# Query features of three tiles made inside the spatial stage, with the weight sums written over their source, and PSUM banks and one sum of the drain taken in another order

## The chip, the cores and the metric

One core of a Trainium2 chip. The metric is the device time of one execution in microseconds (us). The engines are PE (TensorE: matmuls; its weight loads are shown as PEld), DVE (VectorE), ACT (ScalarE), POOL (GpSimd) and SP (SyncE, which here only issues DMAs). Each engine works through its instructions in a fixed order; DMA queues move data beside them.

## The reference

```python
xn = layernorm(x)                                   # 2048 x 512
# A: linear attention with hedgehog features, 32 heads of 16
q, k, v   = xn @ wqkv, by heads
phi(t)    = concat(softmax(t @ w_phi), softmax(-t @ w_phi))
kv, z     = phi(k)^T v,  sum over positions of phi(k)
A         = (phi(q) kv / (phi(q) z + 1e-6)) @ wo
# B: gated MLP over positions
z1, z2    = halves of gelu(xn @ w_in)               # 2048 x 688 each
g         = w_sp @ layernorm(z2) + b_sp             # w_sp: 2048 x 2048
B         = (z1 * g) @ w_out
out       = x + A + B
```

All in fp32. The kernel splits each factor into a high part rounded to the fast matmul type and a low part (the rest), so one product takes three matmuls: L57 (high by high), L58 and L59 (with one low part). `round_h` (L49, ACT) makes the high part and `rest_l` (L53, DVE) the low one.

## The kernel before, in words

The 2048 positions are 16 tiles of 128. The work runs in four stages, and PE goes through them without overlap:

- Projections and k, q features (to about 190 us); e, the exponentials of a query tile with their sums, goes to `e_d` in HBM.
- The second half of `x @ w_in` and its layer norm (to about 290 us).
- **The spatial stage** (about 282 to 489 us): `w_sp @ z2` by Strassen and Winograd. The output is made in 8 pairs of row tiles (`i`, 0 to 7), each from 7 products P1, P2, P6, P5, P7, P3, P4 (in this order, `FORM`). A product adds up in one PSUM bank (`g`) over four steps, quarters of the columns: `n` runs over 32 steps of 42 matmuls. There are 8 banks; a pair holds 7, so P1 of the next pair gets the eighth, its P2 the bank of the old P1, and so on.
- **The final stage** (from 489 us): for each tile `project_u` (u @ w_out into `pout`), for each pair of tiles `attend` (feature transposes, `po`, `oT`) and then `project_o` (oT @ wo, added to `pout`).

For a step, `load_a(n)` loads two blocks of 256 KB of the weights (`wf`, on SP), and `prep_a(n)` makes the four sums S1 to S4 (DVE, L632 to L636, into `S`) and the high and low parts of A11, A12, S1 to S4 and A22 (tiles `A`; ACT L49, DVE L53). Two sets of `A` tiles alternate, so those of step n wait until products of step n − 2 have used them.

At the end of a pair, `drain` empties the seven banks into the tile `c` (ACT L819 copies P1, then DVE L818 to L826), and `gate` applies the gelu to z1 (tile `z1t`, ACT L832), multiplies (L835), splits off a remainder and transposes into the z1 tile (L844, L846), from where 8 DMAs on SP write `u_d` and `ur_d`. The tiles `c` and `z1` have one buffer each. `load_z1` (POOL, L800) brings the next pair's z1 when these writes have landed. After pairs 2 and 4, `c` and `z1` also serve `turn_q`: e of query tile 0 or 1 is loaded into `c` (POOL, L922), transposed by DVE (L579) and written to `q_d`.

`q_fin` turns e of a query tile into its finished features: seven DVE instructions, L563 to L570, which need e and `zb` (the normalizer z, spread over the partitions). Tiles 0 and 1 are finished before the spatial stage, tile 2 in its last steps, and later ones by `features(s)` in the final stage.

`wo` comes in 16 DMAs of 64 KB on SP (L863) and is rounded to `woh` and `wol`.

The order of each engine's instructions is set when the program is built, by a scheduler that takes what can run first; dependences by tile and buffer set the waits. `tc.issue_after` in the code orders one instruction behind another. So code that moves also moves other instructions.

Of the kernel before, what the change touches and what calls it, by code (L numbers as in the profile page):

```python
# [10 lines left out]
F32 = mybir.dt.float32  # L11
# [7 lines left out]
P = 128  # L19
# [22 lines left out]
def mixer(ctx: ExitStack, tc: tile.TileContext, x, x_t, wv, wqkT, phi_bd, wo, w_in, wst, b_r, w_out, out):  # L42
# [557 lines left out]

    def load_a(n):
        i, q = SEQ[n]
        f = []
        for k in range(2):
            t = ws.tile([P, QC, P], F32, tag=f"f{k}", bufs=2, name="wf")
            sp.dma_start(t, wst[2 * i + k, :, q * QC:(q + 1) * QC, :])
            f.append(t.rearrange("p (k two) t -> p two k t", two=2))
        return f

    def prep_a(n, f):  # L610

        a, b = f
        pl = hl[n % 2]
        ops = {}

        tiles = {}
        for names, more in ((("S3", "S4"), 0), (("A22",), 0), (("A11", "A12"), QP), (("S1", "S2"), 0)):
# [11 lines left out]
        sums = (sm[0].tile([P, 4, 2, P], F32, name="S") if sm else  # L629
                zw.tile([P, 4, FC], F32, tag=("T", "z2")[n], bufs=n + 1, name="S").rearrange("p a b -> p (a b)")[:, :8 * P].rearrange("p (a k b) -> p a k b", a=4, k=2))  # L630
        parts(("A11", "A12"), a)
        dve.tensor_tensor(sums[:, 0], b[:, 0], b[:, 1], op=ALU.add)  # L632
        dve.tensor_tensor(sums[:, 1], sums[:, 0], a[:, 0], op=ALU.subtract)  # L633
        parts(("S1", "S2"), sums[:, 0:2])
        dve.tensor_tensor(sums[:, 2], a[:, 0], b[:, 0], op=ALU.subtract)
        dve.tensor_tensor(sums[:, 3], a[:, 1], sums[:, 1], op=ALU.subtract)  # L636
        parts(("S3", "S4"), sums[:, 2:4])
        parts(("A22",), b[:, 1:2])
        return ops

    hl, raw, A, sm = [ws, None], {}, {}, []
    NE = 2
    with ExitStack() as p1:
        tmp1 = p1.enter_context(left("tmp1", 1))
        kvT = tmp1.tile([P, D], F32, name="kvT")
        zb = tmp1.tile([P, NF], F32, name="zb")
        zhl = tmp1.tile([P, 4, D], F32R, tag="zhl", name="zhl")
        psk = p1.enter_context(psum("psk", 2))

        def make_zb():  # L650

            ones_r = tmp1.tile([P, P], F32R, name="ones_r")
            round_h(act, ones_r, ones)
            for k in range(2):
                pz = psk.tile([P, D], F32, tag="kvt", name="pz")
                cs = slice(k * D, (k + 1) * D)
                h, l = (zhl[:, 2 * k + n] for n in range(2))
                round_h(act, h, zacc[:, cs])
                rest_l(l, zacc[:, cs], h)
                pe.matmul(pz, ones_r, h, start=True, stop=False)  # L660
                pe.matmul(pz, ones_r, l, start=False, stop=True)
                dve.tensor_copy(zb[:, cs], pz)

        def make_kvT():
            kvm = zw.tile([P, 4, FC], F32, tag="T", name="kvm").rearrange("p a b -> p (a b)")[:, :D]
# [18 lines left out]
        A[0] = prep_a(0, raw.pop(0))  # L684
        sp.dma_start(kvT_d, kvT)
# [94 lines left out]
    raw[2] = load_a(2)  # L780
    normed(*late.pop(), ins)
    ctx_zw.__exit__(None, None, None)
    ctx_zc.__exit__(None, None, None)
# [9 lines left out]
    sm.append(mid.enter_context(right("S", 1)))  # L793
    ctx_psg = psum("psg", 8)
    psg = ctx_psg.__enter__()

# [17 lines left out]
    def drain(i, g, cb):  # L814
        g = {k: t[:, :FC] for k, t in g.items()}
        b1, b2 = (bias[:, 2 * i + k:2 * i + k + 1] for k in range(2))
        c11, c12, c21, c22 = (cb[:, k, j] for k in range(2) for j in range(2))
        add = lambda o, p, b, q: dve.scalar_tensor_tensor(o, p, b, q, op0=ALU.add, op1=ALU.add)  # L818
        first = act.activation(c12, g["P1"], AF.Copy)  # L819
# [3 lines left out]
        dve.tensor_tensor(c21, g["P7"], c21, op=ALU.add)  # L823
# [76 lines left out]
    for n in range(NC):  # L900
# [4 lines left out]
        if n % NQ == NQ - 1 and i < NP - 1:  # L905
# [1 line left out]
            cq = c[:, :, :FH].rearrange("p k (j f) -> p k j f", j=2)  # L907
            cb = drain(i, g, cq)
            g = {}
        if n + 3 < NC:  # L910
            raw[n + 3] = load_a(n + 3)
        if n + 2 < NC:
            A[n + 2] = prep_a(n + 2, raw.pop(n + 2))
        if n % NQ == NQ - 1 and i < NP - 1:
# [3 lines left out]
            if i in (2, 4):  # L918
# [2 lines left out]
                        for tag, name in (("c", "c"), ("z1", "z1t")))  # L921
                pool.dma_start(e, e_d[s, :, :NF])  # L922
                turn_q(s, t, e, pool)
        if n == NC - 4:
            stage_w()
        if n == NC - 3:
# [30 lines left out]
    def er_pair(name):  # L957
        return cw.tile([P, 2, NF], F32R, tag="er", bufs=3, name=name)

    def features(s):  # L960
# [4 lines left out]
        if s == 3:  # L965
            return
# [6 lines left out]
        e = es[s]  # L973
        if s % 2 == 0:
            ep[s] = er_pair("er")
        es[s] = ep[s - s % 2][:, s % 2]
        lasts[6] = pool.dma_start(es[s].bitcast(F32), e).ins
# [14 lines left out]
    fin.append(last)  # L992
# [43 lines left out]

    def project_u(i, u):
        uh, ul, rt = u
        p = pso.tile([P, D], F32, tag="out", bufs=2, name="pout")
        for c in range(KF):  # L1040
            mm3(p, (uh[:, c], ul[:, c]), wu[c], c == 0, False)
        for k, w in enumerate(wu[KF]):
# [35 lines left out]
            rows = [(m * QP, (m + 1) * QP) for m in range(c // 2 * 8 + c % 2, (c // 2 + 1) * 8, 2)]  # L1078
            load_w(wo, rows, wo_h[:, c], wo_l[:, c], cw.tile([P, D], F32, tag="wof", bufs=4, name="wof"))
    with tc.issue_after(load_w.last):  # L1080
        ets[3] = load_q(3, slot("et"))
        for s in (2, 3):
            us[s] = fetch_u(s)
        ets[4] = load_q(4, slot("et"))

    def ahead(i):

        if i + 5 < NT:
            ets[i + 5] = load_q(i + 5, slot("et"))
        if i + 4 < NT:  # L1090
            with tc.issue_after(brought[i + 2]) if i + 6 >= NT else ExitStack():
                us[i + 4] = fetch_u(i + 4)
        if 3 < i + 3 < NT:
            features(i + 3)

    p, nxt = {}, dict(enumerate(uT))
    for i in range(0, NT, 2):
# [6 lines left out]
            p[i + 1] = project_u(i + 1, nxt.pop(i + 1))  # L1104
        if not i:
            fin.append(lasts[7])
            features(3)
# [51 lines left out]
```

## Time and profile before

| | |
|---|---|
| median of 3 runs | 623.57 us (622.28 to 623.81) |
| profiled execution | 623.54 us, of which the span of the profile is 621.8 us |
| PE busy | 607.6 us (98%) |
| DVE busy | 520.4 us (84%) |
| ACT, POOL busy | 261.3 us (42%), 135.5 us (22%) |
| spatial stage | first product at about 282 us, last one ends at 489.0 us |
| mean clock of PE | 0.991 of full speed |

The profile is of one execution. Rows of the timeline show a start in us from the span's start, a duration, the engine, the line of the kernel, what is written and read, and in brackets the idle time before and what ended it. The lists of waits show how long an engine stood in all, how often and the longest time. Buffer names are those of the program: `g` a product's bank, `c` the drained tile, `A` prepared weights, `wf` raw weights.

### The profile page before, as it was taken

To read this page: it belongs to the slowest core of one execution; us is meant where nothing else is said; L and a number is where in the kernel's file an instruction comes from. 1 tells how busy PE (TensorE), PEld (TensorE's weight loads), DVE (VectorE), ACT (ScalarE), POOL (GpSimd) and SP (SyncE) were. 2 spreads that over 40 slices of the span, in tenths; PEclk is the share of its full clock that TensorE was granted. 3 is DMA by queue.
4 is the path that set the end of the run, shared out by engine and by line. 5 is a ranking of instruction groups with operands and counts; after the bars stand their busy time and mean duration, and the time that the engine had idled before them with its cause. 6 is when DMAs were issued, how large, how long until landed. Compare 5 with 4: busy or idle time off the path is not lost.

```text
span 621.8 us, 11389 instructions
## 1 busy us (share of the span) xinstructions
PE 607.6 (98%) x4286; PEld 551.0 (89%) x4286; DVE 520.4 (84%) x929; ACT 261.3 (42%) x416; POOL 135.5 (22%) x236
## 2 busy tenths in 40 slices
PE   8999999999999999999999999999999799999996
PEld 6888888888889999999999999999999677777775
DVE  5999999999977688888899887697878889999921
ACT  5653334323523657876444442343344333332221
POOL 4122333232110025551000002001000032243420
PEclk9999999999999999999899999999999899999999
DMA  8556875665457847001463755536465799898882
GB/s 310 195 138 164 221 188 160 163 164 155 124 164 209 291 151 253 1 1 37 145 153 114 198 133 177 129 120 184 125 194 158 232 324 324 280 261 250 215 208 58
DMA packets 58414, 109.95 MB, mean 177 GB/s; under 512 B 12456, under 2 KB 24616, under 8 KB 58120
## 3 DMA queue, kind: packets, MB, share of 16 engines
q1 hardware_dynamic: 43400, 64.96, 34.4%
q0 software_dynamic: 12656, 38.64, 24.5%
q10 hardware_dynamic: 2304, 5.64, 2.4%
q8 instruction: 33, 0.54, 0.4%
q14 instruction: 21, 0.17, 0.1%
HBM read 66.85 MB, written 35.80 MB: 165 GB/s over the span
## 4 chain that ended last, share of the span: by engine, by line
PE 77%; DVE 8%; POOL 4%; ACT 4%; issue 3%; DMA 3%; SPq 0%; ACTq 0%; POOLq 0%; DVEq 0%
PE g L57 8%; PE g L58 8%; PE g L59 8%; PE proj L58 7%; PE proj L57 7%; PE proj L59 7%; PE pout L57 6%; PE pout L59 5%; PE pout L58 5%; PE zps L59 3%; PE zps L58 3%; PE zps L57 3%; DVE A L53 1%; POOL rstd L98 1%; PE po L1029 1%
## 5 line engine op out<-in xcount | busy, mean ns | idle before, releaser
L57 PE MATMUL g<-B,A 128*128 128x344 f32 x448 | 142.6, 319 | 2.0 <-ACT A L49 1.1
L58 PE MATMUL g<-B,A 128*128 128x344 f32 x448 | 142.3, 319 | 0.5 <-DVE B L53 0.5
L59 PE MATMUL g<-B,A 128*128 128x344 f32 x448 | 138.5, 318 | 0.2 <-DVE A L53 0.2
L57 PEld LDWEIGHTS g<-B,A 128*128 128x128 f32 x448 | 84.7, 189 | 3.5 <-ACT A L49 1.5
L58 PEld LDWEIGHTS g<-B,A 128*128 128x128 f32 x448 | 84.6, 189 | 0.7 <-DVE B L53 0.7
L59 PEld LDWEIGHTS g<-B,A 128*128 128x128 f32 x448 | 83.7, 189 | 0.5 <-DVE A L53 0.5
L49 ACT ACTIVATE A<-S 128x512 fp32r<-128x512 f32 x64 | 39.4, 629 | 71.0 <-DVE S L633 55.9
L57 PE MATMUL proj<-wqk_h,xT 128*128 128x512 f32 x128 | 50.1, 391 | 0.0
L59 PE MATMUL proj<-wqk_h,xT 128*128 128x512 f32 x128 | 49.8, 389 | 0.0
L58 PE MATMUL proj<-wqk_l,xT 128*128 128x512 f32 x128 | 49.8, 389 | 0.0
L124 ACT ACTIVATE e<-e,r_x 128x1024 f32<-128x1024 f32 x26 | 29.8, 1148 | 42.3 <-DVE e L123 41.2
L53 DVE TENSOR_TENSOR A<-S,A 128x512 fp32r<-128x512 f32 x64 | 42.9, 685 | 3.0 <-ACT A L49 3.0
L49 ACT ACTIVATE A<-wf 128x512 fp32r<-128x512 f32 (+1 forms) x64 | 33.0, 516 | 27.7 <-DMA wf<-in_wst 16.4
L57 PE MATMUL zps<-w1h,xT 128*128 128x344 f32 (+2 forms) x128 | 40.7, 320 | 0.0
L59 PE MATMUL zps<-w1h,xT 128*128 128x344 f32 (+2 forms) x128 | 40.7, 318 | 0.0
L58 PE MATMUL zps<-w1l,xT 128*128 128x344 f32 (+2 forms) x128 | 40.7, 318 | 0.0
L57 PE MATMUL zps<-w2h,xT 128*128 128x344 f32 (+2 forms) x128 | 40.7, 318 | 0.0
L58 PE MATMUL zps<-w2l,xT 128*128 128x344 f32 (+2 forms) x128 | 40.6, 317 | 0.0
L59 PE MATMUL zps<-w2h,xT 128*128 128x344 f32 (+2 forms) x128 | 40.3, 317 | 0.0
L53 DVE TENSOR_TENSOR A<-wf,A 128x512 fp32r<-128x512 f32 (+1 forms) x64 | 35.1, 551 | 4.3 <-ACT A L49 4.3
L127 DVE TENSOR_REDUCE sm<-e 128x64 f32<-128x1024 f32 x26 | 31.1, 1199 | 2.5 <-ACT e L124 2.5
L800 POOL DMA_DIRECT2D z1t<-z_d x16 | 8.7, 552 | 110.0 <-DMA wf<-in_wst 59.3
(222 smaller groups left out, 1441.0 us busy)
## 6 DMA issues: line engine op xcount, KB each, us to landing
wf<-in_wst SPq DMA_DIRECT2D x64, 256.0 KB, 3.5
e_d<-e POOLq DMA_DIRECT2D x16, 544.0 KB, 4.8
et<-e_d SPq DMA_DIRECT2D x16, 544.0 KB, 7.5
z_d<-z1f ACTq DMA_DIRECT2D x16, 344.0 KB, 3.2
z1t<-z_d POOLq DMA_DIRECT2D x16, 344.0 KB, 4.8
zacc<-e POOLq DMA_DIRECT2D x10, 512.0 KB, 4.9
u<-u_d SPq DMA_DIRECT2D x15, 320.0 KB, 5.5
xt<-in_x SPq DMA_DIRECT2D x16, 256.0 KB, 3.8
```

Source lines behind the costliest of these rows:

```text
L49: return act.activation(h, src, AF.Copy).ins
L53: return (eng or dve).tensor_tensor(l, src, h.bitcast(F32), op=ALU.subtract).ins
L57: pe.matmul(dst, ah, bh, start=start, stop=False)
L58: pe.matmul(dst, ah, bl, start=False, stop=False)
L59: return pe.matmul(dst, al, bh, start=False, stop=stop).ins
L98: pool.tensor_tensor(r, mv[:, 1:2], mhalf, op=ALU.pow)
L124: softmax_pair.last = less, act.activation(e, e, AF.Exp, scale=scale).ins
L127: dve.tensor_reduce(sm, heads(e), axis=AX.X, op=ALU.add)
L800: pool.dma_start(t[:, k, :FH], z1_d[2 * i + k])
L1029: lasts[3] = pe.matmul(po[r][c * QP:(c + 1) * QP, k], kvT[rows, m // 2, cols], fs[m // 4][rows, m // 2 % 2], start=True, stop=True).ins
```

## The change

1. After the gate of pairs 1, 3 and 5, the features of query tiles 2, 3 and 4 are made in the tiles `c` and `z1`: POOL loads e into `c` and zb into `z1`, DVE runs `q_fin`, and POOL writes the features back to `e_d`. Tiles 2 and 3 are loaded from there near the end of the spatial stage, tile 4 after it; `q_fin` of tile 2 leaves the last steps, `features(3)` the final stage, and later tiles are finished one tile sooner.
2. The two blocks of raw weights are one tile in three buffers (one in a new pool `fy`, for the former pool `S`), loaded four steps ahead instead of three.
3. The weight sums are written over the raw weights. The order of a step's preparation is now A22, A11 and A12, the sums, S2 and S1, S4 and S3.
4. c22 is made from P7 before c21 is finished, instead of from P5 after.
5. The pool of `pout` is opened ahead of that of the transposes, and the first `pout` is taken at once.

```diff
     def load_a(n):
         i, q = SEQ[n]
-        f = []
+        tag = "fx"[n] if n < 2 else "fyx"[(n - 2) % 3]
+        t = (fy[0] if tag == "y" else ws).tile([P, 2, QC, P], F32, tag="wf" + tag, name="wf")
         for k in range(2):
-            t = ws.tile([P, QC, P], F32, tag=f"f{k}", bufs=2, name="wf")
-            sp.dma_start(t, wst[2 * i + k, :, q * QC:(q + 1) * QC, :])
+            sp.dma_start(t[:, k], wst[2 * i + k, :, q * QC:(q + 1) * QC, :])
...
+        parts(("A22",), b[:, 1:2])
         parts(("A11", "A12"), a)
-        dve.tensor_tensor(sums[:, 0], b[:, 0], b[:, 1], op=ALU.add)
-        dve.tensor_tensor(sums[:, 1], sums[:, 0], a[:, 0], op=ALU.subtract)
-        parts(("S1", "S2"), sums[:, 0:2])
-        dve.tensor_tensor(sums[:, 2], a[:, 0], b[:, 0], op=ALU.subtract)
-        dve.tensor_tensor(sums[:, 3], a[:, 1], sums[:, 1], op=ALU.subtract)
-        parts(("S3", "S4"), sums[:, 2:4])
-        parts(("A22",), b[:, 1:2])
+        a11, a12, a21, a22 = a[:, 0], a[:, 1], b[:, 0], b[:, 1]
+        dve.tensor_tensor(a22, a21, a22, op=ALU.add)
+        dve.tensor_tensor(a21, a11, a21, op=ALU.subtract)
+        dve.tensor_tensor(a11, a22, a11, op=ALU.subtract)
+        dve.tensor_tensor(a12, a12, a11, op=ALU.subtract)
+        parts(("S2", "S1"), pair(a11, a22))
+        parts(("S4", "S3"), pair(a12, a21))
...
         dve.tensor_tensor(c12, g["P5"], c21, op=ALU.add)
+        add(c22, g["P7"], b2, c12)
         dve.tensor_tensor(c21, g["P7"], c21, op=ALU.add)
-        add(c22, g["P5"], b2, c21)
...
-        if n + 3 < NC:
-            raw[n + 3] = load_a(n + 3)
+        if n + 4 < NC:
+            raw[n + 4] = load_a(n + 4)
...
+            elif i % 2 and i < NP - 2:
+                s = NE + i // 2
+                et, t = (gt.tile([P, 2, FU], F32, tag=tag, name=name).rearrange("p k f -> p (k f)")
+                         for tag, name in (("c", "c"), ("z1", "z1t")))
+                pool.dma_start(et[:, :NF + 2 * H], e_d[s])
+                pool.dma_start(t[:, :NF], zb_d)
+                e, _ = q_fin(et[:, :QW], t[:, :NF], t[:, :NF])
+                pool.dma_start(e_d[s, :, :NF], e)
...
-            ets[2] = load_q(2, slot("et"))
-            es[2], last = q_fin(ets.pop(2), slot("qtmp")[:, :NF], zb)
+            for s in (2, 3):
+                es[s] = slot("er", F32R)[:, :NF]
+                sp.dma_start(es[s].bitcast(F32), e_d[s, :, :NF])
...
+    pso = ctx.enter_context(psum("pso", 1))
+    pout = [pso.tile([P, D], F32, tag="out", bufs=2, name="pout")]
     pst = ctx.enter_context(psum("pst", 4))
-    pso = ctx.enter_context(psum("pso", 1))
...
-        if 3 < i + 3 < NT:
-            features(i + 3)
+        if 4 < i + 4 < NT:
+            features(i + 4)
```

What this does to the order. On POOL, in the first pairs of the spatial stage, before (z1t is the tile `z1`; L800 loads z1, L922 and L581 are the turn of query tile 0; the x counts instructions that follow each other):

```order
L770 TENSOR_SCALAR nb<-mv,rstd 128x1
L800 DMA z1t<-z_d 128x688 x6
L922 DMA c<-e_d 128x1024
L581 DMA q_d<-z1t 32x4x256 x4
L800 DMA z1t<-z_d 128x688 x4
```

and now, where L931 and L932 load e and zb, and L934 writes the features back:

```order
L803 DMA z1t<-z_d 128x688 x4
L931 DMA c<-e_d 128x1088
L932 DMA z1t<-zb_d 128x1024
L803 DMA z1t<-z_d 128x688 x2
L934 DMA e_d<-c 128x1024
L925 DMA c<-e_d 128x1024
```

Three transfers through `c` and `z1` now stand between pair 1 and pair 2, with pair 2's load of z1 among them.

On DVE at the end of an even pair, before (L818, L821, L822 and L823 are the drain, L636 and L53 the preparation of the next weights; DMAHW stands for a transfer issued by SP, DMASW for one by POOL):

```order
L818 SCALAR_TENSOR_TENSOR c<-g,bias,c 128x344 [waits PE_49,Activation_49]
L636 TENSOR_TENSOR S<-wf,S 128x256 [waits DVE_49]
L53 TENSOR_TENSOR A<-wf,A 128x2x256 [waits Activation_49]
L821 TENSOR_TENSOR c<-g,c 128x344 [waits PE_49]
L822 TENSOR_TENSOR c<-g,c 128x344 [waits DVE_49,PE_49]
L53 TENSOR_TENSOR A<-S,A 128x2x256 [waits Activation_49]
L823 TENSOR_TENSOR c<-g,c 128x344 [waits DVE_49,PE_49]
```

and now, from the last of the seven instructions of `q_fin` on:

```order
L570 TENSOR_TENSOR c<-c 128x1024 [waits DVE_49]
L53 TENSOR_TENSOR A<-wf,A 128x256 [waits DMAHW6_49,Activation_49]
L635 TENSOR_TENSOR wf<-wf 128x2x128 [waits DVE_49]
L636 TENSOR_TENSOR wf<-wf 128x2x128 [waits DVE_49]
L637 TENSOR_TENSOR wf<-wf 128x2x128 [waits DVE_49]
L638 TENSOR_TENSOR wf<-wf 128x2x128 [waits DVE_49]
L53 TENSOR_TENSOR A<-wf,A 128x2x256 [waits Activation_49] x2
L821 SCALAR_TENSOR_TENSOR c<-g,bias,c 128x344 [waits DMASW2_49,Activation_49]
L824 TENSOR_TENSOR c<-g,c 128x344
```

The drain of pairs 2, 4 and 6 has moved behind the whole preparation of the second step after it, and its first instruction waits for a transfer of POOL, the write of L934; the copy of P1 on ACT waits for it too. Between L563 and L570 stand one sum and three rests of weights.

On PE at the end of the spatial stage, before:

```order
L57 MATMUL g<-B,A 128x344
L58 MATMUL g<-B,A 128x344
L59 MATMUL g<-B,A 128x344
L57 MATMUL pout<-wu,u_uh 128x512 [waits DVE_49,Activation_49]
L58 MATMUL pout<-wu,u_uh 128x512
L59 MATMUL pout<-wu,ul_rt 128x512
```

and now:

```order
L58 MATMUL g<-B,A 128x344
L59 MATMUL g<-B,A 128x344
L57 MATMUL pout<-wu,u_uh 128x512
L58 MATMUL pout<-wu,u_uh 128x512
L59 MATMUL pout<-wu,ul_rt 128x512
```

The first `pout` no longer waits for the drain.

More of the change, by code (lines that the diff above doesn't have):

```diff
@@ L602, in load_a @@
         i, q = SEQ[n]
-        f = []
+        tag = "fx"[n] if n < 2 else "fyx"[(n - 2) % 3]
+        t = (fy[0] if tag == "y" else ws).tile([P, 2, QC, P], F32, tag="wf" + tag, name="wf")
         for k in range(2):
-            t = ws.tile([P, QC, P], F32, tag=f"f{k}", bufs=2, name="wf")
-            sp.dma_start(t, wst[2 * i + k, :, q * QC:(q + 1) * QC, :])
-            f.append(t.rearrange("p (k two) t -> p two k t", two=2))
-        return f
+            sp.dma_start(t[:, k], wst[2 * i + k, :, q * QC:(q + 1) * QC, :])
+        return [t[:, k].rearrange("p (k two) t -> p two k t", two=2) for k in range(2)]
     def prep_a(n, f):
@@ L616, in prep_a @@
         tiles = {}
-        for names, more in ((("S3", "S4"), 0), (("A22",), 0), (("A11", "A12"), QP), (("S1", "S2"), 0)):
+        for names, more in ((("S4", "S3"), 0), (("A22",), 0), (("A11", "A12"), QP), (("S2", "S1"), 0)):
             tiles[names] = pl.tile([P, D * len(names) + more], F32R, tag="".join(names), name="A")
@@ L627, in parts, with pair @@
                 ops[m] = h[:, k], l[:, k]
-        sums = (sm[0].tile([P, 4, 2, P], F32, name="S") if sm else
-                zw.tile([P, 4, FC], F32, tag=("T", "z2")[n], bufs=n + 1, name="S").rearrange("p a b -> p (a b)")[:, :8 * P].rearrange("p (a k b) -> p a k b", a=4, k=2))
+        def pair(x, y):
+            (first, kd, td), more = x.ap, y.offset - x.offset
+            return bass.AP(x.tensor, x.offset, [first, [more, 2], kd, td])
+        parts(("A22",), b[:, 1:2])
         parts(("A11", "A12"), a)
-        dve.tensor_tensor(sums[:, 0], b[:, 0], b[:, 1], op=ALU.add)
-        dve.tensor_tensor(sums[:, 1], sums[:, 0], a[:, 0], op=ALU.subtract)
-        parts(("S1", "S2"), sums[:, 0:2])
-        dve.tensor_tensor(sums[:, 2], a[:, 0], b[:, 0], op=ALU.subtract)
-        dve.tensor_tensor(sums[:, 3], a[:, 1], sums[:, 1], op=ALU.subtract)
-        parts(("S3", "S4"), sums[:, 2:4])
-        parts(("A22",), b[:, 1:2])
+        a11, a12, a21, a22 = a[:, 0], a[:, 1], b[:, 0], b[:, 1]
[5 more added lines that the diff above has]
+        parts(("S4", "S3"), pair(a12, a21))
         return ops
-    hl, raw, A, sm = [ws, None], {}, {}, []
+    hl, raw, A, fy = [ws, None], {}, {}, []
     NE = 2
@@ L684, in mixer @@
         A[0] = prep_a(0, raw.pop(0))
+        raw[2] = load_a(2)
         sp.dma_start(kvT_d, kvT)
@@ L792, in mixer @@
     gt = mid.enter_context(right("gt", 1))
-    sm.append(mid.enter_context(right("S", 1)))
+    fy.append(mid.enter_context(right("fy", 1)))
+    raw[3] = load_a(3)
     ctx_psg = psum("psg", 8)
@@ L958, in er_pair, with into_pair @@
         return cw.tile([P, 2, NF], F32R, tag="er", bufs=3, name=name)
+    def into_pair(s, eng, e):
+        if s % 2 == 0:
+            ep[s] = er_pair("er")
+        es[s] = ep[s - s % 2][:, s % 2]
+        return eng.dma_start(es[s].bitcast(F32), e).ins
     def features(s):
@@ L972, in features @@
             return
[L973 to L977, printed above, removed]
+        lasts[6] = into_pair(s, pool, es[s])
     def gated(u):
@@ L991, in mixer @@
     ctx_psg.__exit__(None, None, None)
-    fin.append(last)
+    fin.append(cb[2])
     sp.dma_start(kvT.rearrange("p g t -> p (g t)"), kvT_d)
+    pso = ctx.enter_context(psum("pso", 1))
+    pout = [pso.tile([P, D], F32, tag="out", bufs=2, name="pout")]
     pst = ctx.enter_context(psum("pst", 4))
-    pso = ctx.enter_context(psum("pso", 1))
     def attend_T(s):
@@ L1038, in project_u @@
         uh, ul, rt = u
-        p = pso.tile([P, D], F32, tag="out", bufs=2, name="pout")
+        p = pout.pop() if pout else pso.tile([P, D], F32, tag="out", bufs=2, name="pout")
         for c in range(KF):
@@ L1080, in mixer @@
     with tc.issue_after(load_w.last):
[L1081 to L1084, printed above, removed]
+        us[2] = fetch_u(2)
+        into_pair(4, sp, e_d[4, :, :NF])
+        us[3] = fetch_u(3)
+        ets[5] = load_q(5, slot("et"))
     def ahead(i):
-        if i + 5 < NT:
-            ets[i + 5] = load_q(i + 5, slot("et"))
+        if i + 6 < NT:
+            ets[i + 6] = load_q(i + 6, slot("et"))
         if i + 4 < NT:
-            with tc.issue_after(brought[i + 2]) if i + 6 >= NT else ExitStack():
+            with tc.issue_after(brought[i + 3]) if i + 6 >= NT else ExitStack():
                 us[i + 4] = fetch_u(i + 4)
-        if 3 < i + 3 < NT:
-            features(i + 3)
+        if 4 < i + 4 < NT:
+            features(i + 4)
     p, nxt = {}, dict(enumerate(uT))
```

4 lines of the change are left out of this document (removed).

## The prediction

> **What bounds the kernel now.** I read the page's engine totals first, then what PE waited for, then the work of each engine by stage, and last the stretches around the places that the change touches.
>
> ```profile
> span 621.8 us, 11389 instructions
> PE 607.6 (98%) x4286; PEld 551.0 (89%) x4286; DVE 520.4 (84%) x929; ACT 261.3 (42%) x416; POOL 135.5 (22%) x236
> ```
>
> PE is the bound: 621.8 − 607.6 leaves 14.2 us in which it does nothing. All the waits of over 0.2 us in the part that the change reaches:
>
> ```profile
> PE pout L57 <- DVE c L823: 4.3, 1, 4.3
> PE g L57 <- ACT A L49: 1.1, 1, 1.1
> PE g L57 <- DVE c L823: 0.9, 2, 0.4
> PE g L58 <- DVE B L53: 0.5, 1, 0.5
> ```
>
> So a gain can come only from about 6.8 us of PE waits and from what a wait costs in clock. DVE is the second engine. The windows give busy us of PE, PEld, DVE, ACT, POOL, then the PE clock, the DMA share and GB/s:
>
> ```profile
> 340.00:380.00 40.00, 40.00 (x263) 40.00 (x262) 32.26 (x69) 15.79 (x27) 3.82 (x7) 1.00 0.55 150
> 380.00:420.00 40.00, 40.00 (x262) 40.00 (x262) 33.96 (x72) 15.62 (x29) 2.16 (x4) 1.00 0.51 145
> 500.00:520.00 20.00, 20.00 (x151) 15.71 (x136) 17.20 (x27) 7.66 (x13) 3.82 (x6) 1.00 1.03 347
> ```
>
> In the spatial stage PE has no hole and DVE is 81 to 85% busy. The final stage (500 on) is bound by PE too, so taking feature work off DVE there gives PE nothing. The question is whether the spatial stage can take the work without stopping PE.
>
> **PE's pace and what a stop costs.** Rows from the timeline: start, duration, instruction, and in brackets the idle time before it.
>
> ```profile
> 487.78 0.32 PE L59 MATMUL g<-B,A 128*128 128x344 f32 x1
> ...
> 488.70 0.31 PE L59 MATMUL g<-B,A 128*128 128x344 f32 x1
> 493.34 0.76 PE L57 MATMUL pout<-wu,u_uh 128*128 128x512 f32 x1 [4.32 <-DVE c L823]
> 498.55 0.39 PE L57 MATMUL pout<-wu,u_uh 128*128 128x512 f32 x1
> ```
>
> ```profile
> 296.89 0.50 PE L57 MATMUL g<-B,A 128*128 128x344 f32 x1 [1.09 <-ACT A L49]
> 297.19 0.49 PE L58 MATMUL g<-B,A 128*128 128x344 f32 x1
> 300.58 0.33 PE L57 MATMUL g<-B,A 128*128 128x344 f32 x1
> ```
>
> Six product matmuls start in 0.92 us: 0.153 us each. A pair of row blocks is 4 steps of 42, so 25.8 us. The last product ends at 489.0, hence pair 1 ended at about 333.5 (489.0 less six pairs of 25.8 and the 0.9 us of waits), and pair 4 at 410.8. After a stop of 4.32 us, matmuls ran slowly from 493.34 to 498.55: 5.2 us at about half pace, 2.4 to 2.6 us lost. After the stop of 1.09 us the pitch was 0.29 us for 3.7 us: 1.7 us lost. Those are my prices for restarting.
>
> The Trainium skill ("TensorE: Matmul & The Clock Gate", "What's actually happening") has the clock halve only after an idle window of about 3.4 us and recover after 3.4 us of work, an estimated 1.7 us lost each time. The stop of 1.09 us cooled the clock all the same, and 5.2 us exceeds one window; by the page the sum below would be about 2 us lower.
>
> **Features in the spatial stage: the cost.** The order of the changed kernel says: the tile's e goes into the one `c` buffer and zb into the one `z1` buffer, both on POOL; DVE makes the features; POOL writes e back from `c`; and the next pair's drain, which starts with ACT's copy of P1 into `c`, waits until that write has landed. The products of the pair behind that (P2, P6 and so on; its P1 has the eighth bank) wait for the banks that this drain empties. The order puts P1 of two of its steps ahead of that wait, so PE has work for 25.8 + 12 × 0.153 = 27.6 us from the end of an odd pair. When has the write landed? Rows of the same links today:
>
> ```profile
> 342.55 0.37 DVE L846 STREAM_TRANSPOSE z1t<-c 128x192 f32<-128x192 f32 x1
> 348.82 1.06 POOL L800 DMA_DIRECT2D z1t<-z_d  x2 [23.89 <-DMA wf<-in_wst]
> 422.40 0.54 POOL L922 DMA_DIRECT2D c<-e_d  x1 [18.45 <-DVE S L632]
> 429.65 1.25 DVE L579 STREAM_TRANSPOSE z1t<-c 128x1024 f32<-128x1024 f32 x1 [3.90 <-DMA wf<-in_wst]
> ```
>
> ```profile
> 486.29 1.23 DVE L563 TENSOR_TENSOR qtmp<-et,zb 128x1024 f32<-128x1024 f32 x1 [0.79 <-PE g L59]
> 489.82 0.57 DVE L818 SCALAR_TENSOR_TENSOR c<-g,bias,c 128x344 f32<-128x344 f32 x1
> 490.31 1.21 DVE L570 TENSOR_TENSOR et<-et 128x1024 f32<-128x1024 f32 x1
> 334.40 0.41 DVE L636 TENSOR_TENSOR S<-wf,S 128x256 f32<-128x256 f32 x1
> 334.73 0.68 DVE L53 TENSOR_TENSOR A<-S,A 128x512 fp32r<-128x512 f32 x1
> 335.33 0.57 DVE L818 SCALAR_TENSOR_TENSOR c<-g,bias,c 128x344 f32<-128x344 f32 x1
> L819 ACT ACTIVATE c<-g 128x344 f32<-128x344 f32 x7 | 3.1, 438 | 0.0
> ```
>
> The transfers, by the list of DMA issues (KB, median us from issue to landing):
>
> ```profile
> e_d<-e POOLq DMA_DIRECT2D x16, 544.0 KB, 4.8
> z1t<-z_d POOLq DMA_DIRECT2D x16, 344.0 KB, 4.8
> er<-et POOLq DMA_DIRECT2D x4, 512.0 KB, 6.4
> zacc<-er POOLq DMA_DIRECT2D x2, 512.0 KB, 4.5
> c<-e_d POOLq DMA_DIRECT2D x2, 512.0 KB, 5.8
> ```
>
> In us from the odd pair's end:
> - The last transpose of the gate ends: pair 1, 342.92 − 333.5 = 9.4; pair 4, where POOL's load follows it, 422.40 − 410.8 = 11.6. I take 10.5.
> - The u writes read z1, so zb can be loaded once they land: 348.82 − 342.92 = 5.9 (7.25 at most, by L579 after its load). The load of e overlaps with this. 16.4.
> - zb lands: 4.8 to 6.4; the nearest row in kind, size and queue is the load of c, 5.8. 22.2. DVE has reached L563 by then and stands there, and the weight tiles of the next two steps queue behind it.
> - The seven instructions L563 to L570: 491.52 − 486.29 less the 0.49 that the L818 between them took is 4.7. The order puts one sum (0.34 apart) and three rounding rests (0.60 apart, by the two rows above) among them: 6.9. 29.1.
> - e goes back: 4.5 to 6.4; nearest is e_d<-e, 4.8. 33.9. ACT's copy of P1, 0.44. 34.3.
>
> PE runs out at 27.6: it stands 6.7 us. With the low ends (9.4 + 5.9 + 4.8 + 4.7 + 4.5 + 0.4 = 29.7) 2.1 us; with the high ends (11.6 + 7.25 + 6.4 + 7.6 + 6.4 + 0.4 = 39.7) 12.1 us. The long stop restarts cold, 2.4 us. This comes three times, in pairs 2, 4 and 6, each chain counted afresh from the end of pairs 1, 3 and 5: **3 × (6.7 + 2.4) = +27.3 us**, between 3 × (2.1 + 1.7) = 11.4 and 3 × (12.1 + 2.4) = 43.5.
>
> The Trainium skill ("DMA: Bandwidth & Descriptors", "Anatomy of one DMA — SWDGE (gpsimd) path") fits 2.0 us plus bytes over 436 GB/s for such a transfer, an estimated 3.2 us for 512 KB. With that for both transfers PE would stand 2.5 us each time, and the sum would come to some 634 us. The rows above show 4.5 to 6.4 us beside this kernel's other traffic, so I don't use it.
>
> **Banks and stage end.** `pout` takes the bank that was free, so the 4.32 us stop and 2.6 us of slow clock go, with q_fin ahead of the drain. What is late next is project_o(0), which needs wo:
>
> ```profile
> 499.80 1.09 PE L1029 MATMUL po<-f,kvT 64*32 64x256 f32 x32
> 500.82 0.50 PE L57 MATMUL pout<-wu,uh 128*128 128x512 f32 x1
> 504.83 0.39 PE L57 MATMUL pout<-woh,oT 128*128 128x512 f32 x1
> 489.48 7.96 SPq L863 DMA_DIRECT2D wof<-in_wo  x16
> 499.05 0.63 ACT L49 ACTIVATE woh<-wof 128x512 fp32r<-128x512 f32 x1 [2.03 <-DMA wof<-in_wo]
> 500.99 1.09 ACT L49 ACTIVATE oT<-po 128x512 fp32r<-128x512 f32 x2 [1.31 <-PE po L1029]
> ```
>
> PE would do project_u(0) in 4.0 us (as 500.82 to 504.83 shows of project_u(1)), po in 1.0, project_u(1) in 4.0: 489.0 + 9.0 = 498.0. SP still issues the 16 loads of wo after the last product, ACT rounds them until 499.7 and then oT, so project_o(0) starts at about 500.8 instead of 504.83: −4.0, after 2.8 us of idling that costs some 1.7 of clock: **−2.3**, between −6.9 (nothing comes back) and 0.
>
> **c22, weight sums in place, wf one step further ahead.** The counts are unchanged (4 sums, 4 roundings, 4 rests a step, two loads of 256 KB), and c22 from P7 frees P5's bank one instruction sooner. In place, A22 is rounded first, into a tile that is released by the last product of two steps before; the sums follow it. Cover: the whole next step, 42 × 0.153 = 6.4 us, plus 1.8 until S2 is used, against 5.1 us of DVE and ACT work in series (4 sums × 0.34, three rests × 0.60, three roundings × 0.63 as that of woh, the same size). Zero while DVE keeps up. At the stage's start the waits of 1.09 and 0.5 us and 1.7 of clock may go or be replaced by others: −0.5, between −3.3 and +0.7. In the final stage DVE gets lighter; PE there has no waits to lose. Zero.
>
> **Sum**, against the profiled execution (623.54 us, within 0.03 of the median 623.57): 623.5 + 27.3 − 2.3 − 0.5 = **648 us**. All low ends: 623.5 + 11.4 − 6.9 − 3.3 = 624.7; all high ends: 623.5 + 43.5 + 0.7 = 667.7.
>
> **Rivals.**
> 1. The write lands in time (faster). It has to land and P1 to be copied by 27.6 us after the odd pair's end, 6.7 sooner than I add up. For it: the low ends come within 2.1 us, and the windows show the DMA engines only half busy. Against it: four transfers in series through the same two buffers, each with a row of 4.5 us or more. Then only stage start and end count: 623.5 − 2.8 = 620.7 (down to 613.3).
> 2. DVE becomes the bound as well. An odd pair gets 4.7 us more, 20.8 (32.26 × 25.8/40) + 4.7 = 25.5 of 25.8 us, and after the stop the drain (7 × 0.5), the gate (by the rows below and its smaller steps about 4) and the next weights (4 × 0.34 + 3 × 0.60 + 0.4) come at once: about 11 us of DVE, while PE has the other 72 matmuls of two steps, 11.0 us. Where ACT and DVE wait for each other some 2 us may stick out each time: 654.
>
> ```profile
> 337.02 1.58 DVE L835 TENSOR_TENSOR c<-z1t,c 128x1376 f32<-128x1376 f32 x1
> 339.32 1.56 DVE L844 STREAM_TRANSPOSE z1t<-c 128x640 f32<-128x640 f32 x2
> ```
>
> 3. The links run near their low ends, stops of 1 to 3 us: about 631. For it: nothing waits long at SP or POOL today. Against: every link has to be short in every pair.
>
> **How the numbers follow.** Chances: forecast 0.60, rival 1 0.17, rival 2 0.13, rival 3 0.10. This kernel's runs tell no change from changes under 0.3%, so the bounds are 621.7 and 625.4. Of rival 1, 0.14 is below 621.7 and 0.03 between; of rival 3 and the forecast's low end 0.03 is between: faster 0.14, same 0.06, slower 0.80. The range 622 to 663 leaves out rival 1's faster part and some 0.05 of the high end; the forecast's own is 636 to 663.
>
> **What would show it.** Right: PE waits `g` <- ACT `c` (the copy of P1) three times, 4 to 10 us, at the ends of pairs 2, 4 and 6, each followed by a few us at half clock; L563 in these pairs idle for some us on a DMA; no stop ahead of the first `pout`, but one ahead of project_o(0). Wrong: no stop in the spatial stage, or stops at other places (on A or B tiles, which would point to the sums in place), or the zb load or e write landing within 3 us.

## The result, and the profile after

The changed kernel took 658.38 us (median of 4, 657.45 to 659.14) beside 623.69 us for the kernel before in the same comparison: a ratio of 1.0558 (95% interval 1.0535 to 1.0580). It is slower by 34.7 us, ten more than the sum, inside the range.

The page of the changed kernel, and what PE waited for there (us in all, times, longest):

```profile
span 657.3 us, 11385 instructions
PE 616.9 (94%) x4286; PEld 558.0 (85%) x4286; DVE 525.4 (80%) x929; ACT 262.2 (40%) x416; POOL 138.7 (21%) x244
```

```profile
PE g L57 <- ACT c L822: 21.0, 3, 7.7
PE g L59 <- DVE A L53: 4.8, 5, 2.2
PE pout L57 <- ACT oT L49: 4.3, 1, 4.3
PE g L57 <- ACT A L49: 2.3, 1, 2.3
```

The first row did not exist before; it is the copy of P1 into `c`, three times, 7.0 us on average. The stop of 4.32 us ahead of the first `pout` is gone, and another of 4.3 us stands ahead of project_o(0), on `oT`. PE idles 40.4 us instead of 14.2, and it is busy 9.3 us longer with the same 4286 matmuls: the clock. By stage (columns as in the prediction):

```profile
340.00:380.00 40.00, 31.73 (x188) 31.17 (x187) 30.28 (x59) 10.98 (x19) 3.22 (x6) 0.87 0.51 147
380.00:420.00 40.00, 40.00 (x260) 40.00 (x259) 31.37 (x65) 15.87 (x28) 4.40 (x8) 1.00 0.61 171
420.00:460.00 40.00, 32.14 (x195) 31.58 (x194) 32.09 (x61) 11.68 (x21) 5.46 (x10) 0.91 0.52 156
460.00:500.00 40.00, 30.91 (x188) 30.35 (x187) 30.92 (x63) 13.43 (x22) 2.68 (x5) 0.90 0.48 147
```

The spatial stage is untouched between the stops (380 to 420); in each of the other stretches lies one. DVE is not busier there than before (30 to 32 us of 40): it waits too. From the first to the last start of a product matmul the stage takes 247.3 us (275.92 to 523.20) instead of 213.0 (275.68 to 488.70; the trace has the first product there, and not at about 282 us): +34.3. From there to PE's last matmul it is 128.4 instead of 127.8: +0.6. So the whole loss is in the spatial stage.

The first stop's chain, link by link, from the timeline (start, duration, instruction, idle time before):

```profile
333.77 0.32 PE L59 MATMUL g<-B,A 128*128 128x344 f32 x1
344.57 0.38 DVE L849 STREAM_TRANSPOSE z1t<-c 128x192 f32<-128x192 f32 x1
352.19 0.53 POOL L932 DMA_DIRECT2D z1t<-zb_d  x1 [6.15 <-DMA wf<-in_wst]
357.91 1.23 DVE L563 TENSOR_TENSOR z1t<-c,z1t 128x1024 f32<-128x1024 f32 x1 [5.85 <-DMA wf<-in_wst]
363.83 1.22 DVE L570 TENSOR_TENSOR c<-c 128x1024 f32<-128x1024 f32 x1
365.34 0.54 POOL L934 DMA_DIRECT2D e_d<-c  x1 [3.37 <-DVE c L570]
369.78 0.46 ACT L822 ACTIVATE c<-g 128x344 f32<-128x344 f32 x1
370.29 0.66 PE L57 MATMUL g<-B,A 128*128 128x344 f32 x1 [7.67 <-ACT c L822]
```

The first row is the last matmul of pair 1 (the 336th of the products), so the pair ended at 334.1. The last transpose ends 10.9 us later (summed with 10.5), zb is asked for 7.2 after that (5.9), L563 starts 5.7 later (5.8), the features end 7.1 later (6.9), and the copy of P1 ends after another 5.2 (4.8 + 0.4): 36.2 us in all instead of 34.3. Two rows name `wf` as releaser, which neither instruction touches. What the zb load waits for, by the code, are the u writes, which read z1 and which SP issued just ahead of loads of `wf`. What L563 still lacks when DVE stands 5.85 us at it is the zb load, issued at 352.19.

### The profile page after: what moved, and what is told of

Read it like the earlier page. It is cut to its first block, busy times and chain, and to the rows that moved or that the text cites. A ratio compares the mean times of both kernels' runs of the same rounds, so it can differ in the third digit from the quotient of the medians.

```text
span 657.3 us, 11385 instructions
## 1 busy us (share of the span) xinstructions
PE 616.9 (94%) x4286; PEld 558.0 (85%) x4286; DVE 525.4 (80%) x929; ACT 262.2 (40%) x416; POOL 138.7 (21%) x244
## 4 chain that ended last, share of the span: by engine, by line
PE 64%; DVE 11%; DMA 9%; issue 6%; ACT 4%; POOL 4%; SPq 2%; ACTq 0%; POOLq 0%; DVEq 0%
PE g L57 7%; PE g L58 7%; PE g L59 7%; PE proj L58 7%; PE proj L57 7%; PE proj L59 7%; PE pout L57 3%; PE pout L59 3%; DMA wf<-in_wst 3%; PE pout L58 3%; PE zps L57 2%; PE zps L59 2%; PE zps L58 2%; DVE A L53 2%; DMA et<-e_d 2%
## 5 line engine op out<-in xcount | busy, mean ns | idle before, releaser
L57 PE MATMUL g<-B,A 128*128 128x344 f32 x448 | 145.2, 327 | 23.4 <-ACT c L822 21.0
L58 PE MATMUL g<-B,A 128*128 128x344 f32 x448 | 145.1, 325 | 0.0
L59 PE MATMUL g<-B,A 128*128 128x344 f32 x448 | 140.3, 326 | 4.8 <-DVE A L53 4.8
L49 ACT ACTIVATE A<-wf 128x512 fp32r<-128x512 f32 (+1 forms) x128 | 70.1, 573 | 138.3 <-PE g L59 58.8
L57 PEld LDWEIGHTS g<-B,A 128*128 128x128 f32 x448 | 87.1, 195 | 24.8 <-ACT c L822 21.9
L59 PEld LDWEIGHTS g<-B,A 128*128 128x128 f32 x448 | 85.6, 194 | 6.7 <-DVE A L53 6.7
L53 DVE TENSOR_TENSOR A<-wf,A 128x512 fp32r<-128x512 f32 (+1 forms) x128 | 77.1, 621 | 14.7 <-ACT A L49 14.3
L58 PEld LDWEIGHTS g<-B,A 128*128 128x128 f32 x448 | 87.2, 195 | 0.0
L57 PE MATMUL pout<-wu,uh 128*128 128x512 f32 x75 | 30.4, 405 | 0.0
L59 PE MATMUL pout<-wu,ul 128*128 128x512 f32 x75 | 29.3, 391 | 0.0
L58 PE MATMUL pout<-wu,uh 128*128 128x512 f32 x75 | 29.2, 390 | 0.0
```

The lines of the kernel that those rows point to most:

```text
L49: return act.activation(h, src, AF.Copy).ins
L53: return (eng or dve).tensor_tensor(l, src, h.bitcast(F32), op=ALU.subtract).ins
L57: pe.matmul(dst, ah, bh, start=start, stop=False)
L58: pe.matmul(dst, ah, bl, start=False, stop=False)
L59: return pe.matmul(dst, al, bh, start=False, stop=stop).ins
```

## The experiments

Times are medians; ratios are to the kernel before, run beside each, with the 95% interval. "Stage" is the time between the first and the last start of a product matmul, "end" the time from there to the start of PE's last matmul; both are of the one profiled execution, and differences of 1 to 2 us between two such columns can be the clock alone (see the last section).

| | us | ratio | stage | end |
|---|---|---|---|---|
| before | 623.7 | 1 | 213.0 | 127.8 |
| changed | 658.4 | 1.0558 (1.0535 to 1.0580) | 247.3 | 128.4 |
| 1 no features | 619.8 | 0.9928 (0.9905 to 0.9951) | 210.3 | 126.1 |
| 2 features only | 658.6 | 1.0559 (1.0536 to 1.0582) | 245.4 | 129.7 |
| 3 own tile for e | 647.5 | 1.0375 (1.0347 to 1.0404) | 237.4 | 128.2 |
| 4 own tile for zb | 656.3 | 1.0524 (1.0490 to 1.0558) | 243.6 | 127.5 |
| 5 DVE work alone | 628.7 | 1.0048 (1.0020 to 1.0076) | 217.2 | 129.0 |
| 6 transfers alone | 627.1 | 1.0045 (1.0021 to 1.0070) | 214.4 | 128.8 |
| 7 two buffers | 633.3 | 1.0149 (1.0119 to 1.0179) | 225.3 | 125.3 |
| 8 banks and c22 | 626.2 | 1.0028 (1.0001 to 1.0054) | 213.7 | 128.9 |
| 9 no write back | 648.7 | 1.0367 (1.0318 to 1.0417) | 236.7 | 127.1 |
| 10 sums and loads | 620.4 | 0.9938 (0.9905 to 0.9971) | 211.5 | 124.4 |
| 11 wo by 4 loads | 631.7 | 1.0084 (1.0050 to 1.0118) | 212.0 | 132.1 |
| 12 wo on two queues | 617.6 | 0.9889 (0.9870 to 0.9908) | 210.5 | 122.4 |

The theory: e and zb pass one after the other through `c` and `z1`, which the gate has just left, and the next drain needs `c`; the chain is longer than a pair. Rival A: the sums in place. Rival B: the queues of DVE and ACT, which have no room for the features. Rival C: the transfers as such.

**1. Without the features.** The new branch of the loop goes, and `load_q(2)`, `q_fin`, `features(3)` and `i + 5`, `i + 3` come back as they were; all else of the change stays.

> The changed kernel without the features in the spatial stage (tiles 2 to 4 are finished where they were before); the sums in place, four loads ahead, c22 and the banks stay. Theory (the one c buffer is held until e is written back): no wait of PE on the copy of P1 into c, no slow clock in the spatial stage, 621 to 626 us. Rival A (the sums in place, with A22's late release, hold PE up): waits on A tiles stay and the time is above 635 us.

Right on the waits; the time, 619.8 us, is 1.2 us under the expected range. PE's waits from the spatial stage on:

```profile
PE g L57 <- ACT A L49: 2.3, 1, 2.3
PE ptq L1018 <- DMA er<-et: 1.5, 1, 1.5
PE pout L57 <- ACT oT L49: 1.5, 1, 1.5
```

No wait on the copy. Rival A is out, and the rest of the change makes the kernel faster by 0.7%.

**2. The features alone**, added to the kernel before (in part; the loads and features of the later tiles move as in the change):

```diff
+            elif i % 2 and i < NP - 2:
+                s = NE + i // 2
+                et, t = (gt.tile([P, 2, FU], F32, tag=tag, name=name).rearrange("p k f -> p (k f)")
+                         for tag, name in (("c", "c"), ("z1", "z1t")))
+                pool.dma_start(et[:, :NF + 2 * H], e_d[s])
+                pool.dma_start(t[:, :NF], zb_d)
+                e, _ = q_fin(et[:, :QW], t[:, :NF], t[:, :NF])
+                pool.dma_start(e_d[s, :, :NF], e)
...
```

> The kernel before with nothing but the features of tiles 2 to 4 in the spatial stage. Theory: three waits of PE on the copy of P1 into c of 6 to 8 us, the slow clock behind each, 650 to 660 us. Rival A (sums in place): below 635 us, since the sums are not in place here.

Right: 658.6 us, the whole loss, though one of the three waits was 4.1 us and not 6 to 8. PE's waits:

```profile
PE g L57 <- ACT c L819: 17.8, 3, 7.6
PE g L59 <- DVE A L53: 8.0, 4, 4.2
```

The two rows make 25.8 us together, as the same two do in the changed kernel (21.0 + 4.8); only the split differs.

**3. A tile of its own for e.** There was room for it only in place of the third raw weight buffer. The edit, in part:

```diff
-        tag = "fx"[n] if n < 2 else "fyx"[(n - 2) % 3]
+        tag = "fx"[n % 2]
...
-        if n + 4 < NC:
-            raw[n + 4] = load_a(n + 4)
+        if n + 3 < NC:
+            raw[n + 3] = load_a(n + 3)
...
-                et, t = (gt.tile([P, 2, FU], F32, tag=tag, name=name).rearrange("p k f -> p (k f)")
-                         for tag, name in (("c", "c"), ("z1", "z1t")))
+                et = fy[0].tile([P, QW], F32, name="et")
+                t = gt.tile([P, 2, FU], F32, tag="z1", name="z1t").rearrange("p k f -> p (k f)")
```

> The changed kernel with a tile of its own for e (where the third raw weight buffer was, so loads go three steps ahead again): c is no longer held by the features; the same DVE work, the same three transfers. Theory: no wait on the copy of P1, 624 to 633 us with small waits on A tiles left. Rival B (the queues: DVE's 4.7 us more per odd pair and the seconds it stands at L563, or ACT's roundings and gelu ahead of the copy): the stops remain at 3 us or more each, 640 to 655 us.

**4. A tile of its own for zb**, with the same two buffers; e stays in `c`.

> The changed kernel with a tile of its own for zb (loads three ahead again): e is still in c and c still waits for the write back, but zb need not wait for the u writes any more, 5 to 7 us less in the chain. Theory: the three waits on the copy of P1 shrink from 7.0 us to 0 to 2.5 us each, 628 to 642 us. Rival B: as long as before, above 650 us.

Both numbers missed (647.5 and 656.3 us), and both lie where rival B had them. PE's waits in 3:

```profile
PE g L57 <- ACT A L49: 9.6, 10, 2.3
PE g L59 <- DVE A L53: 5.2, 3, 2.5
```

and in 4:

```profile
PE g L57 <- ACT c L821: 11.7, 3, 6.9
PE g L57 <- ACT A L49: 8.3, 7, 2.2
```

In 3 the wait on the copy is gone, as the theory said, and no stop is over 2.5 us; in 4 it is about half, where I had expected 0 to 2.5 us each time. But waits on A tiles came, and I had changed two things: the raw weights had lost a buffer. What ACT waited for in 3, from 300 us on, against 0.2 us of this kind in the changed kernel:

```profile
ACT A L49 <- DMA wf<-in_wst: 68.4, 26, 5.5
```

The first wait on the copy in 4 is still 6.9 us. L563 there no longer waits for zb, but for e:

```profile
355.47 1.23 DVE L563 TENSOR_TENSOR zq<-c,zq 128x1024 f32<-128x1024 f32 x1 [1.53 <-DMA c<-e_d]
```

That is 21.4 us after the end of pair 1 (334.1) instead of 23.8. Little is won, because the gate's last transpose ended 15.8 us after the pair instead of 10.9; and the seven instructions then took 9.7 us instead of 7.1, with more of the weights' work among them and 1.4 us of waiting for ACT. So 4 doesn't show what an early zb alone is worth.

**7. Two buffers without features** tells the two apart: experiment 1 with the two edits of `load_a` and the loads from above.

> No features in the spatial stage as in the first experiment, but two raw weight buffers and loads three steps ahead with the sums in place, as in the two kernels with a tile of their own. If their waits on A tiles came from the raw weights being held longer by the sums in place, this has them too: 630 to 645 us, ACT waiting for wf. If they came from the features (DVE standing at L563), this is as fast as with three buffers, 618 to 622 us.

It has them too: 633.3 us, 2.2 points of ratio above experiment 1. ACT and PE in it:

```profile
ACT A L49 <- DMA wf<-in_wst: 71.2, 26, 5.3
...
PE g L57 <- ACT A L49: 8.6, 8, 2.3
PE g L59 <- DVE A L53: 2.9, 3, 1.7
```

The late gate is in 7 too: after pair 1 its last transpose ends 16.9 us after the pair, in 1 it was 10.9. Sums in place hold the raw weights until their last rounding, so with two buffers the next load starts too late. Of experiment 3's loss to experiment 1 (stage +27.1 us), 15.0 are the two buffers. The other 12.1 remain with the features although `c` is free. By its rows, DVE still stands 3.0 to 4.2 us at L563 for zb, and the seven instructions take 10 to 11 us, because parts of the next drain lie among them; which of the two costs how much was not tried.

**5 and 6. The parts alone.** In 5 the seven DVE instructions run on what lies in `c` and `z1`, without the three transfers; in 6 the transfers run without the instructions.

```diff
 5
+                et, t = (y.rearrange("p k f -> p (k f)") for y in (c, z))
+                q_fin(et[:, :QW], t[:, :NF], t[:, :NF])
 6
-                e, _ = q_fin(et[:, :QW], t[:, :NF], t[:, :NF])
-                pool.dma_start(e_d[s, :, :NF], e)
+                pool.dma_start(e_d[s, :, :NF], et[:, :NF])
```

> The changed kernel with the seven DVE instructions of the features run three times on what lies in c and z1, and without the loads of e and zb and the write back (so the features of tiles 2 to 4 are not computed). Theory (transfers and features in series through c and z1, longer than a pair): the chain is 10.5 + 5.9 + 6.9 + 0.4 = 23.7 us, less than 27.6, so no wait on the copy of P1, 618 to 625 us. Rival B (DVE has no room for 4.7 us more per odd pair): stops of 2 us or more at pairs 2, 4 and 6, on A tiles or on the copy, above 635 us.

> The changed kernel with the loads of e and zb and the write back, but without the seven DVE instructions (tiles 2 to 4 are used unfinished). Theory: the write goes out as soon as e is in c and POOL has issued the zb load, 10.5 + 5.9 + 0.6 + 4.4 + 0.4 = 21.8 us, less than 27.6, so no wait on the copy of P1, 618 to 625 us. Rival C (the 1.5 MB of transfers themselves disturb the weights' loads or the u writes): waits on A tiles or on the copy, above 630 us.

628.7 and 627.1 us: a little above what I expected, and below what B (above 635) and C (above 630) said. PE's waits on the copy of P1 are absent in both. In 5:

```profile
PE g L57 <- ACT A L49: 4.6, 3, 2.4
...
PE g L59 <- DVE A L53: 1.2, 2, 1.0
```

and DVE takes the work (busy us of PE, PEld, DVE and so on, as before):

```profile
380.00:420.00 40.00, 40.00 (x261) 40.00 (x261) 37.20 (x78) 16.57 (x29) 3.70 (x7) 1.00 0.50 147
```

37.2 of 40 us, and PE has no hole in this stretch; later, between 455 and 485 us, it stands 3.2 us in three stops. Against experiment 1 the stage grows by 6.9 us with the work alone and 4.1 with the transfers alone, of which 1 to 1.5 us each are the clock at the stage's start, and by 37.0 with both: it is their order one behind the other that costs.

**9. Without the write back.**

```diff
-                e, _ = q_fin(et[:, :QW], t[:, :NF], t[:, :NF])
-                pool.dma_start(e_d[s, :, :NF], e)
+                q_fin(et[:, :QW], t[:, :NF], t[:, :NF])
```

> The changed kernel without the write back of e (tiles 2 to 4 are used unfinished): c is free as soon as L570 has run, the rest of the chain stays. Theory: each wait on the copy of P1 is shorter by the write's landing, 7.0 - 4.3 = 2.7 us, with less slow clock behind it: 637 to 646 us. If ACT's own queue (roundings and gelu ahead of the copy) sets the copy, the waits stay at 5 us or more and the time above 650 us.

648.7 us, between the two. PE's waits:

```profile
PE g L59 <- DVE A L53: 8.6, 3, 5.3
PE g L57 <- ACT c L822: 5.4, 3, 3.0
```

The wait on the copy fell from 21.0 to 5.4 us, more than the write's landing (3 × 4.3); so ACT's queue does not set it. But the waits on A tiles grew from 4.8 to 8.6. The longest of them, 5.34 us until 423.68, stands behind this row:

```profile
419.47 1.23 DVE L563 TENSOR_TENSOR z1t<-c,z1t 128x1024 f32<-128x1024 f32 x1 [5.38 <-DMA z1t<-zb_d]
```

DVE works in its order. While it stands at L563 for zb, the rests of the next steps' weights stand too: ACT's roundings of 414.20 to 415.35 get their rests only from 420.61 on. PE runs out of A tiles first and then meets the bank. So with the write back gone, the late zb still holds PE up.

**8 and 10. What the rest of the change is worth.** 8 is the kernel before with `pout` from the free bank and the new c22; 10 is experiment 1 with the old banks and the old c22.

> The kernel before with the banks and c22 alone. If the gain without the features (624.3 to 619.8 us) is that of the stage's end, this has all of it, 618 to 621 us; if the sums in place and the loads four ahead give part of it, 621 to 623 us.

> The kernel before with the sums in place and the loads four steps ahead alone: old banks, old c22, no features in the spatial stage. The first experiment's spatial stage was 2.7 us shorter than before and its end 1.7 us; banks and c22 alone gave neither. If the spatial stage's part is the sums' and the loads', 620 to 622 us, with the stop of 4 us ahead of the first pout still there; if all of it needs the banks, 623 to 626 us.

8 lies above both of its ranges, 10 in its first one, but with a stop of 1.4 us and not 4. The banks and c22 alone bring nothing (1.0028), the sums in place with loads four steps ahead bring the whole gain (0.9938). In 8 the stop only moves on, from `pout` to `po`; in 10 it shrinks with the old banks. PE's waits at the end of 8, and then that of 10:

```profile
PE po L1030 <- DVE c L818: 2.6, 1, 2.6
PE ptq L1015 <- DMA er<-et: 2.3, 1, 2.3
```

```profile
PE pout L57 <- DVE c L826: 1.4, 1, 1.4
```

The sums in place don't bring it by themselves: in 7, with two buffers and loads three steps ahead, the kernel is slower (1.0149). Whether the third buffer and the earlier loads would bring it with the sums in a tile of their own was not tried.

**11 and 12. A faster version.** With the features out, PE still waits 1.5 us for `oT`, behind the roundings of wo. 11 loads wo by four transfers instead of 16; 12 keeps the 16 and gives every second group of four to POOL. The edits, in part:

```diff
 11
+            load_w.last = sp.dma_start(t, wo.rearrange("(a m two r) d -> a two m r d", m=4, two=2, r=QP)[c // 2, c % 2]).ins
 12
+            load_w(wo, rows, wo_h[:, c], wo_l[:, c], cw.tile([P, D], F32, tag="wof", bufs=4, name="wof"), pool if c % 2 else sp)
```

> The first experiment (no features in the spatial stage, all else of the change) with wo loaded by 4 transfers of 256 KB instead of 16 of 64 KB. SP issued the 16 in 7.7 us and PE stood 1.5 us ahead of project_o(0); with 4 issues of about 0.5 us wo should be there some 5 us earlier and that stop be gone: 616 to 619 us, 0.8 to 1.3% under the kernel before. If a strided load of 256 KB takes as long as the 16, no change from 619.8.

> The first experiment (no features in the spatial stage, all else of the change) with the 16 loads of wo, as they were, shared between SP and POOL, 8 each, since one strided load of 256 KB for four of them landed late (7.6 us of waiting instead of 1.5). If the time of issuing 16 loads on SP (7.7 us) sets when wo is there, both halves are issued in some 4 us, the last rounding of woh comes 2 us earlier or more and the stop of 1.5 us ahead of project_o(0) goes: 616.5 to 619 us, a ratio of 0.988 to 0.992 to the kernel before. If the transfers share a limit behind the queues, the wait stays at 1.5 us or grows and the time is 619.5 to 622.

11 is slower than the kernel before. SP issues the four in 2.77 us, but ACT gets them one by one; SP's row and ACT's roundings:

```profile
486.38 2.77 SPq L1083 DMA_DIRECT2D wof<-in_wo  x4
...
492.16 0.63 ACT L49 ACTIVATE woh<-wof 128x512 fp32r<-128x512 f32 x1 [4.79 <-DMA wof<-in_wo]
495.83 0.63 ACT L49 ACTIVATE woh<-wof 128x512 fp32r<-128x512 f32 x1 [3.04 <-DMA wof<-in_wo]
499.12 0.63 ACT L49 ACTIVATE woh<-wof 128x512 fp32r<-128x512 f32 x1 [2.67 <-DMA wof<-in_wo]
503.84 0.63 ACT L49 ACTIVATE woh<-wof 128x512 fp32r<-128x512 f32 x1 [4.09 <-DMA wof<-in_wo]
```

3.3 to 4.7 us apart. The Trainium skill ("DMA: Bandwidth & Descriptors", "Rules for kernel authors") says that the slowest dimension of a transfer's pattern sets how many of the 16 engines carry it; here that dimension is 4. This would fit, but no run shows the engines of one transfer, and the loads of e and u issued right behind may have slowed these; it stays open. 12 is the best version, 617.6 us, 0.9889 (0.9870 to 0.9908), faster than both kernels:

```profile
489.49 2.19 ACT L49 ACTIVATE woh<-wof 128x512 fp32r<-128x512 f32 x4 [1.77 <-DMA wof<-in_wo]
```

wo is there 5.4 us after the last product (491.68 − 486.28) instead of 11.0 before (499.68 − 488.70), and the stop ahead of project_o(0) is gone.

## Why the prediction was right or wrong

- **The direction and the mechanism were right.** The bank of P1 waits for the write back through `c`, three times, at the places named; the features alone reproduce the whole loss (2), and without them it is gone (1).
- **The chain was 2 us too short**: 34.3 us summed; 36.2, 35.9 and 37.2 measured from the ends of pairs 1, 3 and 5 (334.1, 397.3 and 459.5). Two links were off. The gate's last transpose came 10.9 to 12.1 us after the pair (10.5), and zb was asked for 7.2, 7.2 and 8.7 us after that (5.9). The first of them I had misread already: counting back from the stage's end I put the ends of pairs 1 and 4 of the kernel before at 333.5 and 410.8, but their last matmuls start at 331.77 and 409.13, so the gate took 10.8 and 13.0 us there, and not 9.4 and 11.6.
- **The stops**: by these chains PE has nothing to do for 3 × (36.4 − 27.6) = 26.4 us, where I summed 20.1. The waits show 25.2 of it: 21.0 on the copy and 4.2 on A tiles just ahead. That 21.0 lies near 20.1 is luck.
- **The slow clock behind the stops**: 3 × 2.4 = 7.2 summed. The stretches at half pace were 5.3, 3.9 and 5.3 us (370.29 to 375.6, 433.24 to 437.1, 496.73 to 502.0); at a pitch of 0.287 instead of 0.153 that is 6.8 us. The price came from a single stop; it held for these three long ones, but shorter stops often cost nothing (last section). The row of the first:

```profile
370.29:375.60 5.31, 5.31 (x18) 5.31 (x19) 5.24 (x9) 1.26 (x2) 0.00 (x0) 0.50 0.34 99
```

- **A wait without a price.** I wrote that the weight tiles of the next steps queue behind L563, and gave that no price. PE waited for them 4.2 us in the three pairs (0.60, 1.35 and 2.24). Here this adds nothing, since PE would have stood until the copy in any case: the two waits make 25.8 us in 2 as in the changed kernel, with 8.0 and 4.8 of them on A tiles. It has a price as soon as the chain gets shorter, as in 9. Rival 2 had DVE as the bound after the drain; it was DVE standing still before the drain, and 5 shows that the work itself nearly fits.
- **The end of the stage**: −2.3 summed, +0.6 measured. The bank did remove the stop of 4.3 us. But project_o(0) started 13.6 us after the last product, where I summed 11.8, since wo came later:

```profile
523.20 0.32 PE L59 MATMUL g<-B,A 128*128 128x344 f32 x1
...
536.85 0.80 PE L57 MATMUL pout<-woh,oT 128*128 128x512 f32 x1 [4.34 <-ACT oT L49]
523.97 9.56 SPq L866 DMA_DIRECT2D wof<-in_wo  x16
534.95 1.36 ACT L49 ACTIVATE woh<-wof 128x512 fp32r<-128x512 f32 x2 [2.35 <-DMA wof<-in_wo]
```

  SP took 9.56 us to issue the 16 loads, not 7.96, and a stop of 4.34 us, not 2.8, was followed by the slow clock again. That what was late next would take most of the gain back was right; that some is left was not, and 8 says the same of the banks without the features.
- **Sums, loads and c22 at zero**: wrong for the sums and loads. Alone they bring 3.6 us (10). The profile of before showed DVE waiting for `wf` in the stage (7.9 us at L632, three times) and the stop behind the drain at its end. I took the first for hidden and did not ask what an earlier DVE would do to the second.
- **The stage's start**: −0.5 summed, +1.8 measured (57.9 us to the last matmul of pair 1 instead of 56.1). One stop of 2.28 us (on an A tile) stands where two of 0.45 and 1.09 us did.
- Of the 34.3 us in the stage, the longer waits make 25.4 (28.1 after: 21.0 + 4.8 + 2.3; 2.7 before) and the clock behind the three stops 6.8; 2.1 us I can't assign. Of the ten us between sum and result, 6.3 are the chains, 2.3 the stage's start and 2.9 its end; the clock takes back 0.4, and another 0.7 that went the other way I can't assign.

## What to carry to other kernels

When work is put into a stage that the bound engine fills, ask not for the room of the engine that does it, but for the buffers that it borrows: list each transfer in series through them, and set the sum against the time until the owner wants them back. Price what queues behind every instruction that waits for a DMA, also where the engine has plenty of room on average; a longer wait can hide it (in the changed kernel) and its end bring it out (in 9). And before a stop at a stage's end is removed, look up what is late next; here, in the changed kernel, the loads of wo took back what the free bank had given.

## What was not expected of the hardware

The same stop of PE does not always cost clock. At the stage's start PE stands 2.38 us in 10 and 2.41 us in 12, at the same place. The stretches of equal length behind these stops, 10 first (columns as above, the clock third from the end):

```profile
294.72:298.44 3.72, 3.72 (x12) 3.31 (x13) 3.69 (x7) 2.79 (x6) 0.00 (x0) 0.54 0.71 258
294.47:298.19 3.72, 3.57 (x21) 3.23 (x22) 3.69 (x7) 2.80 (x6) 0.00 (x0) 1.00 0.73 249
```

The kernel before ran at a slow pitch for 3.7 us, losing 1.7, after stops of 0.45 and 1.09 us close together; 8 has stops of 0.43 and 1.08 us at the same place and kept the full clock. Experiment 7 has eleven stops, up to 2.29 us (8.6 + 2.9 us in all); the mean granted clock of its profiled execution was 0.999, that of the other three 0.989 to 0.997. Where the clock falls during the work, it stays at half for 3.41 us or for two, three or four times as long (6.8 us behind the stop of 4.32 us in the kernel before, 10.2 behind the first stop of the changed one). What decides whether a short stop costs clock stays open. The rule of an idle window of 3.4 us (the Trainium skill, "TensorE: Matmul & The Clock Gate", "What's actually happening") fits the short stops that cost nothing; the slow stretches behind stops of 1.09 and 2.38 us it does not explain.

And the same 1 MB of wo in four transfers instead of 16 came later by far (11), though it was issued in about a third of the time.
